# Linear attention followed by a gated long convolution, one core: more crossbar transposes, other eviction engines, shared buffer pools and a rewritten instruction order

## The chip, the cores and the metric

The program runs on one core of one Trainium2 chip. The metric is the device time of one execution in microseconds; the median of three runs of the kernel before is 264.32 us. Its profile is one execution recorded by the hardware profiler. The engines are TensorE (PE for its matmuls, PEld for its weight loads), VectorE (DVE), ScalarE (ACT), GpSimd (POOL) and the sync engine (SP); the last two mostly issue transfers here.

## What is computed

For 8 batches, 8 heads, 576 positions and a head size of 64, attention is replaced by positive random features; its output, with the heads side by side as 512 columns, goes into a gated convolution along the positions, done as a Fourier transform over 576 points:

```python
q_p, k_p = phi(q * scale), phi(k * scale)      # exp(x @ omega.T - |x|^2/2 - max) / sqrt(128)
kv  = einsum('bhsm,bhsd->bhmd', k_p, v)
z   = sum(k_p, axis=2)
num = einsum('bhsm,bhmd->bhsd', q_p, kv)
den = einsum('bhsm,bhm->bhs', q_p, z)[..., None] + 1e-06
x   = (num / den).transpose(0, 2, 1, 3).reshape(8, 576, 512)

x1, x2, x3 = split(x @ w_proj, 3)
conv = irfft(rfft(x2, axis=1) * rfft(filter, axis=0), n=576, axis=1)
out  = (x1 * conv * x3) @ w_out
```

## The kernel before

**Tiling.** A batch has 512 "main" positions, four blocks of 128, and 64 "left" positions; the left ones of two batches share a block of 128. The eight batches are so handled as four pairs. The function `attention` writes down the first half of the work for all batches, `hyena` the second half for all pairs. The 576-point Fourier transform is done by matmuls with tables of sines, after a fold that splits it into three.

**How one batch goes through.** Keys, queries and values come from DRAM through GpSimd's queue and are cast to bf16 on the way (`load_main`, `load_left`; tiles kn, qn, vn, kl, ql, vl). Keys and queries must be turned, so that the head dimension lies across partitions: kn becomes kt, qn becomes qt. There are two ways. Either TensorE multiplies 128x128 blocks with an identity, eight into one PSUM bank, and VectorE or ScalarE copies the bank out (`transposes`, `turn_keys`, `turn_queries`); or one DMA with transposition, issued on SP, moves the whole tile through the crossbar (`cross`). The table `CROSSED` (line 24) says from which batch on the second way is taken: 5 for keys, for queries and for the attention output. Then TensorE multiplies with omega and ScalarE takes the exponential (ek for keys, eqt for queries). VectorE takes each key row's maximum over the features and scales the values by it (`max_to_c`, `scale_values`; vc). TensorE sums keys times values to kv, multiplies the queries with it, VectorE divides (`normalise`; xb), and the result is turned back to xt: by TensorE and a ScalarE copy (`turn_back`, `turn_runs`), or through the crossbar.

**Second half.** xt is folded on VectorE (`fold`; xf), projected (`project2`, `gates`; tiles x and x13), transformed (`forward`; xs and sp, with `sw` and `xw` as copies whose partition halves are swapped by SP transfers), multiplied with the filter's spectrum (`spectrum`; ha, hb, hps, hqs), transformed back (yt) and multiplied with w_out; the results osb go out through SP.

**The filter.** It is loaded by GpSimd (`load_filter`), folded by seven VectorE additions and subtractions (`fold_filter`), transformed by TensorE (`filter_transform`) and put into place by SP transfers (`split_out`). The spectrum of the first batch needs it.

**Order.** Nothing is issued as it is written down. The class `Plan` records every operation; consecutive matmuls into the same tile form one. At the end `issue` (line 226) emits them in the order of the list of numbers `ORDER` (line 26), which fixes the order on each engine and in each transfer queue. Every engine works its own queue in order; a waiting instruction holds all behind it. GpSimd's queue has up to eight transfers under way: each waits for the one eight places ahead of it.

**Buffers.** Each tile name has its own ring of buffers in one of the pools `nat`, `att`, `hy` (qn 2, xt 4, x13 3, and so on); a tile that takes over a buffer waits until the last user of the former one is done. PSUM has eight banks: two pairs named a (`two_banks`), three single ones named h (`bank`) and one named t (`bank_t`) for transposes.

In the profile every instruction has line 232, the line that emits it, so groups are told apart by tile names.

Of the kernel before, what the change touches and what calls it, by code (L numbers as in the profile page):

```python
# [12 lines left out]
FP32 = mybir.dt.float32  # L13
BF16 = mybir.dt.bfloat16
# [7 lines left out]
P = 128  # L22

CROSSED = {"keys": 5, "queries": 5, "out": 5}

ORDER = """
    0 28 138 55 1 29 30 136 32 2 33 26 35 4 137 27 3 5 37 31 56 11 38 39 10 22 44 7 48 45 8 49 46
    50 6 40 52 15 23 51 34 24 84 13 139 41 42 20 47 70 43 21 71 36 77 69 85 25 9 53 86 54 73 57 72
    75 87 585 587 82 588 58 59 589 63 88 61 12 74 60 64 62 89 66 90 96 91 78 17 68 92 65 97 76 67
    93 98 95 80 211 586 107 99 106 109 100 142 148 108 110 81 79 149 112 101 150 154 94 14 152 102  # L30
    151 155 590 153 103 156 104 158 157 214 594 105 159 219 111 180 141 593 181 164 114 113 19 160
    165 16 115 182 161 116 184 117 162 183 118 122 163 18 119 123 120 222 124 216 121 125 210 126
    170 127 172 628 171 223 173 623 624 128 146 215 166 174 626 129 212 224 591 176 629 130 213
    592 140 167 644 226 175 596 597 595 625 630 131 627 168 177 225 144 132 169 637 645 133 651
    178 632 639 134 646 143 642 179 654 135 185 638 598 228 631 652 643 186 187 227 633 218 601
    599 640 655 229 188 641 602 191 189 603 192 600 647 193 605 650 604 190 635 194 606 607 195
    145 653 196 230 666 609 217 231 197 608 198 147 611 610 282 232 612 83 199 287 233 250 615 200
    613 201 205 251 202 616 617 252 614 203 619 206 204 618 207 288 621 620 289 253 718 254 208
    291 255 209 290 719 720 292 665 221 294 622 722 293 295 667 296 669 724 297 670 298 234 721
    671 347 235 299 656 236 246 237 304 673 247 659 305 674 248 306 672 681 307 286 249 683 238  # L40
    352 657 684 257 658 320 284 239 682 240 256 241 687 321 308 686 258 309 689 685 649 358 690
    260 648 359 688 663 242 244 259 243 661 245 691 350 262 264 692 662 660 694 318 265 664 357
    364 261 319 285 365 263 322 668 283 300 675 323 324 269 676 677 270 271 301 266 703 267 701
    268 704 693 274 678 272 275 702 276 277 679 707 273 636 278 279 709 634 708 696 280 710 705
    360 695 281 680 723 711 706 362 810 220 346 302 341 355 303 361 342 726 343 479 363 697 344
    353 367 811 345 366 829 813 699 368 351 424 725 370 348 698 815 814 700 356 728 712 371 738
    816 741 349 740 713 743 714 739 473 311 812 369 749 474 744 754 750 742 745 752 751 746 755
    313 817 753 756 310 818 747 314 382 757 312 727 758 716 316 315 782 386 317 785 729 783 715
    325 328 788 383 329 326 418 327 731 786 387 354 789 830 333 330 730 790 717 336 732 331 784
    337 334 338 734 332 335 426 736 388 372 733 339 428 735 389 340 390 427 791 391 373 881 429  # L50
    374 375 430 828 792 431 376 832 384 883 793 787 833 377 433 834 421 379 485 378 380 836 819
    432 423 737 400 420 835 434 837 419 846 385 820 844 748 759 435 847 450 760 451 436 850 845
    437 495 851 392 438 852 496 822 831 853 439 761 824 823 821 762 763 825 826 764 401 381 765
    854 827 477 771 394 448 855 476 766 773 475 857 772 838 767 768 774 856 839 769 776 449 452
    775 393 777 864 453 454 778 840 779 780 866 841 468 865 842 797 469 395 470 794 867 798 396
    868 397 795 471 849 800 472 848 872 869 801 562 398 796 882 799 873 886 843 884 399 802 858
    870 563 425 781 402 859 405 871 885 406 407 889 403 887 874 888 413 891 890 404 803 414 892
    878 408 893 770 409 415 410 894 895 860 862 804 411 913 412 805 861 416 879 915 806 417 863
    896 917 483 875 488 918 487 481 914 919 876 807 880 422 489 920 809 916 922 484 921 490 897
    923 482 877 491 899 924 898 925 480 493 928 900 478 931 929 926 440 930 441 933 932 442 939  # L60
    934 944 941 935 942 940 927 936 443 444 937 901 943 446 445 1008 945 961 903 486 1009 946 447
    950 947 953 989 962 458 455 951 459 992 963 938 456 952 990 457 902 993 954 991 461 994 460
    1007 464 462 995 996 463 465 955 466 997 497 904 467 492 905 494 948 956 906 498 957 808 964
    907 908 513 965 514 909 966 536 970 507 911 516 967 1011 508 910 968 1012 515 969 1060 912 971
    999 518 958 517 1062 1064 509 972 519 510 1015 1010 520 959 1013 1066 539 1016 538 1061 540
    976 1014 1063 541 949 973 998 1000 977 542 499 543 974 978 1001 500 544 501 502 504 1005 503
    511 1002 512 979 1006 545 1023 1003 1024 546 980 982 1004 981 960 547 1025 983 1029 506 548
    1026 1031 1030 505 1027 549 1019 1028 1032 550 521 537 1020 551 985 522 1033 526 984 986 560
    1038 1022 1034 975 1068 1037 561 1021 1039 523 1070 1017 524 527 525 1065 1018 528 529 1067
    532 1069 530 531 1072 533 534 552 1074 1036 535 553 1041 1073 554 1040 1071 1043 555 1042 1035  # L70
    1096 987 1075 1044 557 556 1098 1101 1097 1099 558 1102 1107 1100 1112 1109 1103 564 1108 1110
    559 1113 1045 1111 1049 565 1104 1114 1051 566 1115 1046 1105 567 570 1052 568 1047 1092 1116
    1050 988 1169 1140 569 1094 1048 1170 573 1141 1143 574 575 1142 1146 1168 571 580 572 1147
    1171 581 1148 582 576 1172 1173 577 578 583 1057 1174 1093 579 1144 1058 1149 1095 1175 1106
    1150 1187 584 1151 1076 1176 1188 1059 1077 1078 1053 1118 1079 1081 1120 1190 1119 1191 1080
    1186 1178 1177 1192 1082 1083 1194 1054 1084 1195 1055 1193 1056 1202 1179 1086 1204 1203 1121
    1205 1123 1122 1207 1129 1117 1124 1134 1206 1130 1131 1125 1132 1145 1135 1210 1133 1085 1136
    1211 1126 1137 1208 1087 1088 1127 1209 1189 1089 1090 1216 1128 1180 1091 1182 1138 1181 1212
    1158 1213 1152 1159 1139 1215 1183 1217 1160 1155 1153 1218 1184 1154 1156 1214 1157 1196 1185
    1198 1161 1199 1197 1201 1239 1162 1200 1164 1241 1163 1230 1165 1224 1231 1219 1222 1225 1220  # L80
    1228 1221 1223 1275 1226 1229 1280 1276 1167 1232 1240 1277 1227 1281 1278 1243 1279 1242 1244
    1245 1282 1283 1286 1246 1247 1287 1237 1288 1248 1249 1233 1251 1235 1234 1250 1271 1236 1252
    1273 1238 1253 1272 1254 1289 1274 1291 1290 1297 1292 1256 1299 1293 1298 1284 1255 1294 1295
    1259 1257 1258 1319 1285 1296 1325 1320 1261 1322 1328 1323 1326 1324 1300 1329 1302 1301 1330
    1308 1303 1313 1310 1327 1304 1260 1309 1166 1314 1311 1321 1262 1264 1305 1312 1263 1315 1307
    1316 1267 1306 1265 1318 1266 1268 1269 1331 1270 1317 1332 1335 1334 1333 1338 1336 1337 1341
    1339 1340 1344 1342 1343 1345 1346 1348 1347
# [148 lines left out]
def kernel(  # L236
# [39 lines left out]
    def bank():  # L276
        return nc.tile(psum, [P, 512], FP32, name="h", bufs=3)

    def bank_t():
        return nc.tile(psum, [P, 512], FP32, name="t", bufs=1)  # L280
# [4 lines left out]
    def load_main(b, which, parts=1, between=None):  # L285
        nc.at("load " + which, b)
        if which == "q" and b >= NS:

            t_ = nc.tile(nat, [P, NT, H, D], BF16, name="qn", bufs=2)
            nat_tiles[which, b] = t_  # L290
            for t in range(NT):
                nc.gpsimd.dma_start(
                    out=t_[:, t], in_=q[b, :, t * P : (t + 1) * P].rearrange("h s d -> s h d")
                )
            return
        src = {"q": q, "k": k, "v": v}[which]
        t_ = nc.tile(nat, [P, H, NT, D], BF16, name=f"{which}n", bufs=2)
# [11 lines left out]
    def load_left(i, which):  # L309
        nc.at("load " + which + "l", 2 * i)  # L310
        src = {"q": q, "k": k, "v": v}[which]
        t_ = nc.tile(nat, [P, H, D], BF16, name=f"{which}l", bufs=1)
        for j in range(2):
            nc.gpsimd.dma_start(
                out=t_[j * SL : (j + 1) * SL, :, :],
                in_=src[2 * i + j, :, SM:S, :].rearrange("h p d -> p h d"),
            )
        nat_tiles[which + "l", i] = t_
# [1040 lines left out]
```

The softmax here doesn't subtract the row's maximum and nothing guards it: scores larger than these inputs give would overflow.

## Time and profile before

| | |
|---|---|
| runs of the kernel before | 264.32, 263.89, 265.74 us; median 264.32 |
| span of the profiled execution | 264.5 us |
| granted TensorE clock, mean | 0.987 |
| DMA packets | 86786, 35.26 MB |
| GpSimd's queue (loads) | 59616 packets, 17.31 MB |
| SP's queue | 27000 packets, 17.47 MB |
| crossbar transposes | 9, some 4.4 us from issue to landing |
| loads of 512 KB by GpSimd | 8.2 to 11.5 us from issue to landing |
| ScalarE table loads | 2, 1283 ns each |

The busy time of an engine is the time in which one of its instructions ran; matmuls overlap, so that a TensorE that is always busy may still hold more or less work. The chain of waits follows back from the last instruction, at each step to what released it. In lists of groups, the numbers after the bar are the summed time, the mean of one instruction in ns, and the engine's idle time just ahead of them with what ended it. Times in the timeline are in us from the start of the span.

### The profile page before, as it was taken

How to read it: one execution, taken by the hardware profiler on the slowest of the kernel's cores; microseconds unless marked ns; L12 is line 12 of the kernel's file. 1: busy time of each engine (PE TensorE's matmuls, PEld its weight loads, DVE VectorE, ACT ScalarE, POOL GpSimd, SP SyncE). 2: the span in 40 equal slices, each digit the busy share in tenths (PEclk: the TensorE clock that was granted, in tenths of full speed). 3: DMA queues.
4: the chain of work that ended last, by engine and by line, in shares of the span. 5: the costliest groups of instructions: out<-in, count | busy, mean ns of one | idle time of the engine just before them, and what ended most of it. 6: DMA issues, size and time to landing. Idle time of an engine off the chain costs nothing.

```text
span 264.5 us, 5749 instructions
## 1 busy us (share of the span) xinstructions
PE 243.5 (92%) x2250; PEld 138.2 (52%) x2250; DVE 211.6 (80%) x474; ACT 194.0 (73%) x308; POOL 63.0 (24%) x88
## 2 busy tenths in 40 slices
PE   0665969999999999999999999999999999999994
PEld 0443836565476647655456454446456554456541
DVE  6896795689968999999399897599989889279480
ACT  4796579758999997987958967996495654763533
POOL 7865652902360912313017000000000000000000
PEclk9998699999999999999999999999999999999999
DMA  7999999999999999998579958416444511520136
GB/s 68 164 187 197 195 201 189 185 196 177 84 181 142 133 144 145 171 182 55 128 173 136 116 121 174 124 42 151 125 85 141 121 41 41 178 59 2 46 132 198
DMA packets 86786, 35.26 MB, mean 133 GB/s; under 512 B 58219, under 2 KB 81256, under 8 KB 86760
## 3 DMA queue, kind: packets, MB, share of 16 engines
q0 software_dynamic: 59616, 17.31, 64.2%
q1 hardware_dynamic: 27000, 17.47, 26.3%
q8 instruction: 17, 0.28, 0.4%
q10 hardware_dynamic: 144, 0.13, 0.1%
q14 instruction: 9, 0.07, 0.1%
HBM read 34.64 MB, written 9.44 MB: 167 GB/s over the span
## 4 chain that ended last, share of the span: by engine, by line
PE 77%; DMA 7%; DVE 6%; ACT 5%; issue 2%; POOL 1%; SPq 1%; DVEq 0%; POOLq 0%
PE h L232 60%; PE a L232 13%; PE t L232 4%; DMA vl<-in_v_dram 4%; DMA qn<-in_q_dram 3%; ACT ek L232 2%; SPq L232 1%; DVE x L232 1%; DMA xw<-xr 1%; DVE xb L232 1%; DVE kt L232 1%; ACT qt L232 1%; POOL kn L232 1%; ACT x L232 1%; DVE yt L232 1%
## 5 line engine op out<-in xcount | busy, mean ns | idle before, releaser
L232 PE MATMUL h<-xt,wproj 128*128 128x512 bf16 x256 | 62.8, 380 | 0.0
L232 ACT CAST x<-h 128x512 bf16<-128x512 f32 x68 | 40.0, 596 | 25.9 <-PE h L232 25.7
L232 PEld LDWEIGHTS <-wproj 128*128 128x128 bf16 x384 | 31.0, 98 | 25.5 <-issue 1.1
L232 ACT ACTIVATE eqt<-a 128x1024 bf16<-128x1024 f32 x32 | 32.2, 1040 | 3.5 <-PE a L232 3.5
L232 ACT ACTIVATE osb<-h 128x512 f32<-128x512 f32 (+4 forms) x49 | 27.2, 571 | 10.0 <-PE h L232 7.3
L232 ACT ACTIVATE ek<-a 128x1024 bf16<-128x1024 f32 x32 | 32.1, 1040 | 3.1 <-PE a L232 3.1
L232 POOL DMA_DIRECT2D qn<-in_q_dram x26 | 23.1, 894 | 40.4 <-PE t L232 16.0
L232 PE MATMUL h<-wproj,xf 128*128 128x512 bf16 x128 | 31.7, 379 | 0.0
L232 DVE TENSOR_TENSOR x<-h,x 128x512 bf16<-128x512 f32 x32 | 22.0, 687 | 11.8 <-PE h L232 10.1
L232 PE MATMUL h<-wout,yt 128*128 128x512 bf16 x128 | 30.9, 379 | 0.3 <-DVE yt L232 0.3
L232 DVE TENSOR_TENSOR bt<-h,osb 128x384 f16<-128x384 f32 x32 | 17.0, 551 | 6.7 <-PE h L232 6.1
L232 PEld LDWEIGHTS <-yt 128*128 128x128 bf16 x128 | 11.9, 98 | 14.1 <-DVE yt L232 1.0
L232 PE MATMUL h<-x,fwb 128*128 128x512 bf16 x72 | 18.7, 379 | 0.0
L232 PEld LDWEIGHTS <-xf 128*128 128x128 bf16 x134 | 12.2, 98 | 12.3 <-issue 0.2
L232 DVE TENSOR_TENSOR xb<-a,rden 128x512 bf16<-128x512 f32 x24 | 16.3, 688 | 0.5
L232 PE MATMUL h<-gtab,xs 128*128 128x384 bf16 x64 | 15.6, 326 | 0.1
L232 PE MATMUL a<-om,kt 64*128 64x128 bf16 x256 | 11.8, 226 | 3.7 <-DVE kt L232 3.7
L232 PEld LDWEIGHTS <-eqt 128*128 128x128 bf16 x256 | 11.4, 99 | 6.4 <-DVE xb L232 1.0
L232 PE MATMUL a<-kv,eqt 128*128 128x65 bf16 x256 | 12.6, 195 | 0.4 <-DVE xb L232 0.2
L232 PE MATMUL a<-qt,om 64*128 64x512 bf16 x64 | 11.4, 390 | 1.5 <-ACT ek L232 0.7
L232 PEld LDWEIGHTS <-kt 64*128 64x128 bf16 x256 | 7.8, 98 | 8.7 <-DVE kt L232 5.0
L232 PE MATMUL a<-vc,ek 128*128 128x65 bf16 x256 | 11.9, 200 | 0.0
(157 smaller groups left out, 475.8 us busy)
## 6 DMA issues: line engine op xcount, KB each, us to landing
out_dram<-osb SPq DMA_DIRECT2D x24, 256.0 KB, 2.3
vn<-in_v_dram POOLq DMA_DIRECT2D x8, 512.0 KB, 9.2
kn<-in_k_dram POOLq DMA_DIRECT2D x7, 512.0 KB, 8.7
qn<-in_q_dram POOLq DMA_DIRECT2D x24, 128.0 KB, 7.0
sw<-sp SPq DMA_DIRECT2D x16, 128.0 KB, 2.5
wproj<-in_moe_w_proj_dram POOLq DMA_DIRECT2D x3, 512.0 KB, 11.5
qn<-in_q_dram POOLq DMA_DIRECT2D x2, 512.0 KB, 8.2
out_dram<-xf SPq DMA_DIRECT2D x4, 256.0 KB, 2.2
```

Of the source, the lines that this page charges most:

```text
L232: getattr(real, name)(*args, **kw)
```

## The change

- `CROSSED` becomes 3 for keys and queries and 2 for the output: five batches of keys and queries and six of the output go through the crossbar instead of three each.
- All queries that TensorE still turns (batches 0, 1 and 2) are copied out of PSUM by ScalarE. Before, VectorE did it for batches 0 and 1.
- The seven additions and subtractions of `fold_filter` are issued on GpSimd instead of VectorE.
- The identity is made by VectorE, by comparing two ramps, instead of by GpSimd.
- The named rings of the pools are replaced by three shared rings: m4 (22 buffers of 4 KB per partition), m2 (10 of 2 KB) and m1 (19 of 1 KB). The bank t is given to h, which has four.
- `ORDER` is a new list, 1329 operations instead of 1349.

```diff
-CROSSED = {"keys": 5, "queries": 5, "out": 5}
+N4, N2, N1 = 22, 10, 19
+
+CROSSED = {"keys": 3, "queries": 3, "out": 2}
...
     def bank():
-        return nc.tile(psum, [P, 512], FP32, name="h", bufs=3)
+        return nc.tile(psum, [P, 512], FP32, name="h", bufs=4)
...
     def bank_t():
-        return nc.tile(psum, [P, 512], FP32, name="t", bufs=1)
+        return nc.tile(psum, [P, 512], FP32, name="h", bufs=4)
...
-        t_ = nc.tile(nat, [P, H, NT, D], BF16, name=f"{which}n", bufs=2)
+        t_ = nc.tile(hy, [P, H, NT, D], BF16, name="m4", bufs=N4)
...
         iota(si[:, 0 : 2 * CH], pattern=[[1, 2 * CH]], base=0, channel_multiplier=0)
-        nc.opaque("POOL", lambda: make_identity(tc.nc, ident[:]), ident[:], 650.0)
+        iota(fp[:], pattern=[[0, 1]], base=0, channel_multiplier=1)
+        nc.vector.tensor_scalar(
+            out=ident[:], in0=si[:, 0:P], scalar1=fp[:, 0:1], scalar2=None, op0=ALU.is_equal
+        )
...
-            nc.vector.tensor_tensor(out=x[:, o], in0=x[:, y], in1=x[:, z], op=op)
+            nc.gpsimd.tensor_tensor(out=x[:, o], in0=x[:, y], in1=x[:, z], op=op)
...
-                kt = nc.tile(att, [P, H, 2, P], BF16, name="kt", bufs=1)
-                qt = nc.tile(att, [P, NT, NPAIR, P], BF16, name="qt", bufs=1)
+                kt = nc.tile(hy, [P, H, 2, P], BF16, name="m4", bufs=N4)
+                qt = nc.tile(hy, [P, NT, NPAIR, P], BF16, name="m4", bufs=N4)
...
-                        b >= 2,
+                        True,
...
-                xt = nc.tile(hy, [P, CB, SM], BF16, name="xt", bufs=4)
+                xt = nc.tile(hy, [P, CB, SM], BF16, name="m4", bufs=N4)
```

All other tiles of one, two and four KB change their pool and name in the same way. In the instruction streams that result, TensorE has 2138 matmuls instead of 2250, VectorE no copies of turned queries, and GpSimd's queue has the filter's folds between its loads: four after the load of the filter's main part, the other three in places among the next twelve loads. SP's queue has the first five crossbar transposes (keys of batches 3 and 4, queries of 3, output of 2, keys of 5) ahead of or among the filter's placing and the first swaps.

## The prediction

> **What bounds the kernel now.** I read the page's busy table, slices and chain first, then busy time by stretch, then the chain in order of time, the groups kept apart by shape, and the queues.
>
> ```profile
> PE 243.5 (92%) x2250; PEld 138.2 (52%) x2250; DVE 211.6 (80%) x474; ACT 194.0 (73%) x308; POOL 63.0 (24%) x88
> PE   0665969999999999999999999999999999999994
> PE 77%; DMA 7%; DVE 6%; ACT 5%; issue 2%; POOL 1%; SPq 1%; DVEq 0%; POOLq 0%
> ```
>
> TensorE is full from the seventh slice (40 us) to the last, and 77% of the chain is its own. So there are two things to buy: less TensorE work, and an earlier moment from which it is full. By stretch (columns: stretch, length, PE, PEld, DVE, ACT, POOL busy, granted clock, DMA share, GB/s):
>
> ```profile
> 0.00:10.00 10.00, 1.01 (x6) 0.57 (x7) 7.43 (x32) 4.94 (x9) 8.67 (x20) 1.00 0.87 93
> 20.00:30.00 10.00, 6.99 (x103) 5.67 (x101) 6.41 (x13) 6.32 (x8) 5.82 (x8) 0.70 1.42 198
> 30.00:35.00 5.00, 3.76 (x54) 2.47 (x52) 4.55 (x11) 1.54 (x3) 2.54 (x4) 0.92 1.60 192
> 35.00:40.00 5.00, 3.83 (x31) 1.73 (x33) 4.92 (x17) 5.00 (x7) 2.94 (x4) 1.00 1.30 202
> 40.00:45.00 5.00, 4.99 (x80) 3.90 (x79) 2.25 (x4) 4.95 (x10) 1.77 (x2) 1.00 1.60 190
> ```
>
> Up to 40 us TensorE idles while VectorE is the busy engine (9.5 of the 10 us from 30 to 40) and the DMA engines move a steady 190 to 200 GB/s. Prices on TensorE come from the chain, start to start:
>
> ```profile
> 46.90 1.73 PE h L232 x8
> 76.90 0.46 PE t L232 x8
> 181.19 1.26 PE a L232 x40
> ```
>
> That is 216 ns for a product 512 columns wide, 56 for a transpose, 31.5 for one of 65. With 32.5 ns for key features (x8 0.26), 163 and 83 ns for 384 and 192 columns (timeline), the 2250 matmuls weigh 730 x 0.216 + 304 x 0.0555 + 640 x 0.0315 + 288 x 0.0325 + 128 x 0.0555 + 96 x 0.163 + 64 x 0.083 = 232.1 us. I call the clock minus the weight issued so far the **lag**. In this timeline
>
> ```profile
> 45.35 0.81 PE L232 MATMUL h<-wproj,xf 128*128 128x512 bf16 x3
> ```
>
> is the first projection; 20.2 us of weight stand ahead of it, so the lag is 25.1. The first output product (97.3) has 69.6 ahead: 27.7. The last (260.5) has 231.9: 28.6. The span is 232.1 + 28.6 + 3.8 of tail = 264.5, 0.2 from the runs' median of 264.32, so I use one for the other. Nearly all lag is made in the first 45 us.
>
> **What the skill says.** "TensorE: Matmul & The Clock Gate" (Wait — 56ns, not 53.3ns?) gives 55.6 and 215.7 ns from start to start at 128 and 512 columns, warm; the chain's 56 and 216 agree. "Advanced Engine Details and Errata" (X-Bar Transpose (TRN2)) calls crossbar transposes as fast as plain DMAs, 350 to 400 GB/s; the trace's take 4.4 us to land 512 KB, some 120 GB/s with their latency, and I use the trace. "GPSIMD Engine Reference" (3.1 Elementwise; 8. Key points) has a two-input add of 2048 fp32 at 4497 ns on GpSimd, and its SBUF interface shared with VectorE. No run here shows that; from it I estimate 1.12 us for 512 columns, more beside a busy VectorE.
>
> **The change, part by part.** *Transposes.* Keys and queries of batches 3 and 4, outputs of 2, 3 and 4 leave TensorE: seven sets of 16, 112 matmuls x 0.0555 = 6.2 us. TensorE is full there, so all counts: weight 225.9. Their evictions go too, off engines with room:
>
> ```profile
> L232 DVE COPY kt<-t 128x1024 bf16<-128x1024 bf16 x10 | 6.8, 684 | 1.4 <-PE t L232 1.4
> L232 ACT COPY qt<-t 128x1024 bf16<-128x1024 bf16 x6 | 6.3, 1056 | 0.0
> L232 DVE COPY qt<-t 128x1024 bf16<-128x1024 bf16 x4 | 2.7, 686 | 1.3 <-PE t L232 1.3
> L232 ACT COPY xt<-t 128x1024 bf16<-128x1024 bf16 x6 | 6.1, 1021 | 2.1 <-PE t L232 2.1
> L232 DVE TENSOR_TENSOR yt<-yt 128x512 bf16<-128x512 bf16 x5 | 2.0, 414 | 0.0
> ```
>
> VectorE loses 4 kt copies, 4 qt copies and 7 folds of 0.41: 8.4 us. ScalarE loses 6 xt copies, trades 4 late qt copies for 4 early ones.
>
> *Start.* Identity moves from GpSimd (TensorE's first wait, until 6.9) into VectorE's queue behind the residues: first transpose near 9.5. In the new stream ScalarE loads tables three times (1.28 each), one now behind a VectorE value. First exponential: 14.0, against 12.54. From there to the last turned block of batch 0 ScalarE has 17 exponentials x 0.90, 5 copies x 0.93, 9 short ones x 0.49 (chain and timeline spacings) = 24.4, plus about 1 waiting for the values of batch 0, which land some 3 us later in the new order: 39.5. The first third of wproj stands behind 5376 KB instead of 5056, so at 37 instead of 23.77 + 11.5 = 35.3. First projection at 40, with 18.1 ahead: lag 21.9, a gain of 3.2.
>
> *Filter fold.* In the new order TensorE's first filter product stands at weight 32.1 (54.0 at lag 21.9) and waits for the third of three folds on GpSimd. Their load has 2496 KB more ahead of it than wproj's third, at 190 GB/s 13.5 us: lands at 50.5. With f per fold it waits until 50.5 + 3f. While GpSimd waits and folds it issues no load. Behind stand six issues (5.2 us), a fold, an issue, the keys of batch 4, two folds, two issues, and the last piece of queries 3: issued at 50.5 + 6f + 8.6, landed 7.0 later (page), crossed 4.4 later, 70.5 + 6f; TensorE takes them at weight 55.7. So that path asks a lag of 14.8 + 6f: 21.5 at f = 1.12, 24.4 at 1.6, 28.3 at twice the estimate. VectorE is near full then; I take f = 1.6. Bounds: 0.8 (twice VectorE's 0.41; nothing excludes that it hides) and 2.25.
>
> *Crossings and SP.* Sixteen instead of nine, the first five of them (keys 3 and 4, queries 3, output 2, keys 5) among the filter's stores and the sw, xw swaps on SP:
>
> ```profile
> 88.93 6.56 SPq L232 DMA_TRANSPOSE kt<-kn  x1
> 133.06 1.87 SPq L232 DMA_TRANSPOSE qt<-qn  x1
> ```
>
> One held SP 6.6 us with GpSimd issuing, one 3.3, the later seven 1.3 to 2.2. Keys 4 can go at 70; at 3.3 each keys 5 are out near 83, then fifteen small moves x 0.6 end at 92, landing by 95; VectorE has them in its queue ahead of what TensorE wants at weight 72.9 (97). Covered, by 2 us; without that cover it is a stall of the excess.
>
> *Pools.* No instruction. They add waits: values 4 now wait for keys 5 to be crossed, a piece of queries 6 for TensorE at weight 83; both hold GpSimd's queue, values 4 land near 93 and are used after 110. One PSUM bank more for h, shared with t: ScalarE has one more to run ahead, I count nothing.
>
> Sum: 225.9 + lag + 3.8. The lag starts at 24.4; before, it still grew by 3.5 after the first projection, by waits on evictions and small gaps. I add 2, since part of that now hides in the fold's wait: **256.1**. With no growth and no wait 225.9 + 21.9 + 3.8 = 251.6; with f = 2.25 and 3 more, 261.
>
> **Rivals.** *The crossings take the gain back (no change).* If the first ones each hold SP 6.6 us because GpSimd is loading: keys 4 go at 70, output 2 leaves at 90 instead of being there at weight 58.7 (83): 7 us, lag 31.5 and 1 more, 262.2. For it: the 88.93 line, and a DMA share of 1.3 to 1.8. Against: the other eight took 3.3 or less.
>
> *GpSimd holds the loads (slower).* The same 14.8 + 6f: at f = 3.3 it asks 34.6, and 225.9 + 34.6 + 3.8 = 264.3, the point from which it decides; at f = 4, 38.8 and 268.5. For it: a queue in order, in front of all loads, and a VectorE 4.6 to 4.9 of 5 us busy. Against: it needs three times the page's price.
>
> *The new order does nothing for the start.* ScalarE is the only busy engine there; Some 3 us more there and the lag is 25.1 as before: 225.9 + 28.6 + 3.8 = 258.3, the transposes alone.
>
> **Numbers.** Forecast and the start rival, both faster: 0.72 and 0.09. Crossings, no change: 0.11. GpSimd, slower: 0.08. 1% is 2.6 us, about what a measurement tells from none. Range 251.5 to 263: from no growth to the crossings' case.
>
> **What will show it.** 2138 matmuls; first projection at 40 (45.35 before); TensorE waiting for GpSimd near 54; fold durations against 1.6; sixteen DMA_TRANSPOSE, the first six near 1.9 to 3.3 each; lag at the end below 28. Wrong if a stretch after 60 us shows TensorE idle by several us before kt, qt or xt.

## The result, and the profile after

The change makes the kernel **slower**: 268.85 us median (268.12 to 269.41 in three runs, 274.74 in the profiled one) against 264.12 us for the kernel before in the same session. The ratio is 1.0143, with a 95% interval of 1.0096 to 1.0191. The forecast was 256.1 us, with a range up to 263.

The lines of the page that answer to those shown of before, from the profiled execution of the kernel after:

```profile
PE 238.2 (87%) x2108; PEld 132.7 (49%) x2138; DVE 207.1 (76%) x460; ACT 190.1 (70%) x303; POOL 72.8 (27%) x94
PE   0477799988998929999966999999999999999993
PE 68%; DMA 10%; DVE 8%; ACT 8%; issue 2%; SPq 1%; ACTq 0%; DVEq 0%
```

That execution took 274.74 us at a mean clock of 0.965, so the readings below are from a second trace of the same kernel (run a0: 268.18 us, span 266.4, clock 0.977). Its slices of TensorE:

```profile
PE   0477799996999939999999899999999999999993
```

TensorE is full from the sixth slice on, one earlier than before, as wanted, but now the tenth slice (60 to 67 us) drops to 6 and the fifteenth (93 to 100 us) to 3. TensorE's share of the chain falls from 77% to 68 or 66%. A sum that is 6.2 us lighter takes longer because TensorE waits in the middle, where before every slice read 9. The stretches of run a0 (columns: stretch, length, PE, PEld, DVE, ACT, POOL busy, clock, DMA share, GB/s) give both ends of the story:

```profile
35.00:40.00 5.00, 5.00 (x88) 3.85 (x86) 2.90 (x6) 4.83 (x8) 2.29 (x4) 1.00 1.24 205
...
60.00:65.00 5.00, 2.95 (x11) 0.94 (x9) 4.94 (x8) 2.89 (x4) 5.00 (x5) 0.80 1.74 162
95.00:100.00 5.00, 0.25 (x2) 0.00 (x0) 0.96 (x2) 1.56 (x3) 2.41 (x3) 1.00 1.39 222
```

From 60 to 65 us VectorE (4.94) and GpSimd (5.00) are both full while TensorE has 2.95. From 95 to 100 us no engine is: they wait for something that is not an engine.

The forecast's own measure, the lag (clock minus TensorE's weight so far; where the trace misses matmuls, the program's list is used, so that these figures hold to some 0.3 us), puts a size on each part:

| | before | forecast | after (a0) |
|---|---|---|---|
| first projection (45.35; after 40.3 us) | 25.1 | 21.9 | 22.2 |
| at 60 us | 26.1 | 24.4 | 23.8 |
| at 70 us | 27.1 | | 27.9 |
| at 90 us | 27.7 | | 29.3 |
| at 110 us | 28.5 | | 35.6 |
| last output product | 28.6 | 26.4 | 36.0 |

225.9 + 36.0 + 4.5 of tail = 266.4, against 256.1. At 60 us the change was ahead of its forecast. Then it lost 4.1 us near 63, 1.4 between, and 6.3 near 100.

**The first loss.** VectorE and GpSimd in the timeline of run a0 (columns: start, duration, engine, operation, count, and the idle time ahead with what ended it):

```profile
53.17 2.69 DVE L229 TENSOR_TENSOR m<-m 128x1024 bf16<-128x1024 bf16 x2
...
60.47 1.63 DVE L229 TENSOR_TENSOR vcl<-m,vcl 64x512 bf16<-64x512 bf16 x1
```

```profile
50.25 5.33 POOL L229 TENSOR_TENSOR m<-m 128x512 bf16<-128x512 bf16 x3 [3.48 <-DMA m<-in_moe_filter_fft_dram]
...
60.61 1.21 POOL L229 TENSOR_TENSOR m<-m 128x512 bf16<-128x512 bf16 x1
```

The GpSimd lines are filter folds. The VectorE lines are ordinary work, and they are too long: the first line is two operations, one of 1024 columns and one of 512 (a line shows the shape of its first), which take 1.03 us in e4, not 2.69; the multiplication of the left values takes 0.42, not 1.63. Note 1.63 = 0.42 + 1.21: it took its own time plus one fold on GpSimd. TensorE then waits for VectorE:

```profile
59.61 1.04 PE L229 MATMUL h<-wproj,m 128*128 128x512 bf16 x4
62.70 1.63 PE L229 MATMUL h<-wproj,m 128*128 128x512 bf16 x4 [2.05 <-DVE m L229]
64.12 1.91 PE L229 MATMUL h<-m,wproj 128*128 128x512 bf16 x4
```

Four products take 1.04 us ahead of the gap, and 1.63 and 1.91 behind it. The wait is 2.05 us long by the profile's ends of matmuls, and 2.2 counted from the four products' weight, 4 x 0.216; both counts occur below, some 0.2 us apart. The lag grows by 4.1.

**The second loss.** SP's queue and ScalarE, same run:

```profile
72.19 12.18 SPq L229 DMA_TRANSPOSE m<-m  x3
84.42 0.58 SPq L229 DMA_DIRECT2D hps<-m  x1
85.11 2.18 SPq L229 DMA_TRANSPOSE m<-m  x1
...
91.49 1.31 SPq L229 DMA_DIRECT2D hqs<-m  x2
...
98.16 0.60 SPq L229 DMA_DIRECT2D hqs<-m  x1
```

```profile
98.44 0.58 ACT L229 CAST m<-h 128x512 bf16<-128x512 f32 x1 [5.36 <-DMA hqs<-m]
```

Four crossbar transposes hold SP from 72 to 87 us, and the filter's placing (hps, hqs) stands between and behind them until 98.8. ScalarE waits 5.36 us for it: its copy takes over a buffer of the shared ring m2 that the placing still reads. VectorE waits 3.97 us, because its products need hps. Behind ScalarE's copy stands the last exponential of the queries, and so TensorE idles 4.75 us up to 100.0. The move that ScalarE waits for is the second of the two issued from 91.49 us on; it landed at 98.3, some 6 us later. The pages say the same of such moves (medians from issue to landing, of the kernel before and of run a0):

```profile
hqs<-osb SPq DMA_DIRECT2D x4, 64.0 KB, 6.2
hqs<-m SPq DMA_DIRECT2D x4, 64.0 KB, 6.0
```

### The profile page after: what moved, and what is told of

Its sections match the earlier page's. It is cut to its first block, busy times and chain, and to the rows that moved or that the text cites. A ratio compares the mean times of both kernels' runs of the same rounds, so it can differ in the third digit from the quotient of the medians.

```text
span 273.0 us, 5512 instructions
## 1 busy us (share of the span) xinstructions
PE 238.2 (87%) x2108; PEld 132.7 (49%) x2138; DVE 207.1 (76%) x460; ACT 190.1 (70%) x303; POOL 72.8 (27%) x94
## 3 DMA queue, kind: packets, MB, share of 16 engines
q1 hardware_dynamic: 41560, 21.14, 34.2%
## 4 chain that ended last, share of the span: by engine, by line
PE 68%; DMA 10%; DVE 8%; ACT 8%; issue 2%; SPq 1%; ACTq 0%; DVEq 0%
PE h L229 57%; PE a L229 11%; DMA m<-m 8%; DVE m L229 6%; ACT ek L229 3%; DMA hqs<-m 2%; ACT m L229 2%; ACT eqt L229 2%; SPq L229 1%; DVE vcl L229 1%; ACT L229 0%; DVE rden L229 0%; DVE eql L229 0%; DVE mx L229 0%; ACT kv L229 0%
## 5 line engine op out<-in xcount | busy, mean ns | idle before, releaser
L229 ACT CAST m<-h 128x512 bf16<-128x512 f32 (+1 forms) x132 | 72.1, 583 | 48.0 <-PE h L229 40.1
L229 PEld LDWEIGHTS <-m 128*128 128x128 bf16 (+2 forms) x983 | 71.0, 101 | 67.1 <-DVE m L229 14.8
L229 PE MATMUL h<-m,wproj 128*128 128x512 bf16 (+1 forms) x373 | 74.6, 335 | 4.7 <-DMA m<-m 4.3
L229 ACT ACTIVATE m<-h 128x512 f32<-128x512 f32 (+4 forms) x57 | 32.2, 570 | 13.6 <-PE h L229 12.2
L229 PE MATMUL h<-wproj,m 128*128 128x512 bf16 x138 | 37.4, 391 | 2.3 <-DVE m L229 2.0
L229 POOL DMA_DIRECT2D m<-in_q_dram x34 | 28.7, 860 | 27.1 <-DVE bt L229 20.6
L229 PE MATMUL h<-wout,m 128*128 128x512 bf16 x136 | 35.0, 384 | 0.7 <-issue 0.3
L229 DVE TENSOR_TENSOR m<-m 128x512 bf16<-128x512 bf16 (+3 forms) x52 | 27.2, 533 | 5.7 <-DMA m<-m 4.7
L229 DVE TENSOR_TENSOR m<-h,m 128x512 bf16<-128x512 f32 x36 | 24.5, 681 | 7.6 <-PE h L229 7.3
L229 POOL DMA_DIRECT2D m<-in_v_dram x16 | 12.7, 798 | 45.8 <-PE h L229 25.1
L229 DVE TENSOR_TENSOR bt<-h,m 128x384 f16<-128x384 f32 x32 | 16.9, 553 | 10.4 <-ACT m L229 8.6
L229 DVE TENSOR_TENSOR m<-a,rden 128x512 bf16<-128x512 f32 x36 | 24.2, 684 | 0.6
```

Source lines behind the costliest of these rows:

```text
L229: getattr(real, name)(*args, **kw)
```

## The experiments

Ratios are to the kernel before, timed beside each; 0.38% is 1 us. All kernels start from the kernel after unless another is named.

| run | ratio | 95% interval |
|---|---|---|
| a0 | 1.0162 | 1.0096 to 1.0228 |
| e1_fold_vector | 1.0185 | 1.0115 to 1.0255 |
| e2_moves_off_sp | 1.0109 | 1.0078 to 1.0141 |
| e3_queries5_first | 1.0213 | 1.0139 to 1.0288 |
| f1_no_more_crossings | 1.0346 | 1.0309 to 1.0384 |
| f3 (f1, with e1 and e2) | 1.0397 | 1.0354 to 1.0440 |
| g1_late_pieces | 1.0299 | 1.0265 to 1.0334 |
| b1_before_fold_gpsimd | 1.0248 | 1.0211 to 1.0285 |
| b2_before_queries_scalar | 1.0010 | 0.9990 to 1.0031 |
| e4_fold_vector_later | 1.0113 | 1.0034 to 1.0192 |
| h2 (e4 and e2) | 1.0068 | 1.0023 to 1.0114 |
| h1 (h2 and g1) | 0.9923 | 0.9889 to 0.9957 |
| h1 again | 0.9915 | 0.9880 to 0.9949 |
| d1 (h1 and idle work on GpSimd) | 1.0036 | 1.0011 to 1.0060 |
| i1 (h1, two edits) | 0.9996 | 0.9956 to 1.0037 |
| i2 (i1, one more) | 0.9978 | 0.9950 to 1.0006 |
| i3 (i2 without i1's moved folds) | 0.9875 | 0.9814 to 0.9935 |
| i4 (h1 and i2's edit) | 0.9985 | 0.9956 to 1.0015 |

**a0: does it belong to the kernel?**

> The changed kernel once more, for a trace whose granted clock is near 1. If the three idle stretches of TensorE seen in its first trace (2.2 us near 60 us before a projection that waits for VectorE, 5.3 near 95 us before sums that wait for ScalarE, 4.4 near 140 us behind a crossbar transpose) belong to the kernel, they are here again within 1 us and the time is 268. If they came with the low clock of that execution (0.965), they are gone and the time is below 262.

The first two stretches are there again, 2.2 and 4.9 us counted from the weights. The third is not: it came with that execution, and nothing below explains it.

**b1: the fold alone, in the kernel before.**

```diff
-            nc.vector.tensor_tensor(out=x[:, o], in0=x[:, y], in1=x[:, z], op=op)
+            nc.gpsimd.tensor_tensor(out=x[:, o], in0=x[:, y], in1=x[:, z], op=op)
```

> The kernel before with its seven filter folds on GpSimd and nothing else changed. Theory, a fold there takes 1.2 to 1.8 us and VectorE's bf16 work beside it 1.3 us instead of 0.4, in a stretch in which VectorE is full, and the loads behind the folds are later: 266 to 270. Rival, the fold hides: 263.5 to 265.

271.17 us, 6.6 more by the ratio: one word costs more than the whole change does. The timelines of VectorE, GpSimd and TensorE in this run:

```profile
38.01 4.49 DVE L232 TENSOR_TENSOR vc<-vn,vc 128x2048 bf16<-128x2048 bf16 x1 [0.42 <-DMA vn<-in_v_dram]
```

```profile
38.21 1.17 POOL L232 TENSOR_TENSOR yt<-yt 128x512 bf16<-128x512 bf16 x1
...
40.02 1.16 POOL L232 TENSOR_TENSOR x<-x 128x512 bf16<-128x512 bf16 x1
...
41.83 2.79 POOL L232 TENSOR_TENSOR yt<-yt 128x512 bf16<-128x512 bf16 x2
```

```profile
41.23 0.59 PE L232 MATMUL h<-x,fwar 128*128 128x512 bf16 x1 [4.16 <-POOL x L232]
```

TensorE waits 4.16 us for a fold, and VectorE's scaling of the values takes 4.49 us where its group has a mean of 1.22 in the kernel before. So two prices lie on top of each other: the fold's result comes late, and VectorE is held. The next two experiments part them.

**e1 and e4: the folds back on VectorE.** In e1 at the same places of `ORDER`; in e4 four of them (603, 606, 605, 607) behind operation 580.

```diff
-            nc.gpsimd.tensor_tensor(out=x[:, o], in0=x[:, y], in1=x[:, z], op=op)
+            nc.vector.tensor_tensor(out=x[:, o], in0=x[:, y], in1=x[:, z], op=op)
```

> The seven filter folds go back to VectorE, at the same places of the order. Theory one, the folds on GpSimd cost twice, once by slowing VectorE's bf16 work beside them (1.3 us instead of 0.41 for 512 columns) and once by holding the loads of keys 4 and 5 behind them: VectorE's work is at its usual durations, the keys of batch 4 are issued some 5 us earlier, the idle stretch near 60 us is gone and the one near 95 us is shorter; 261 to 265. Rival, the crossings on SP's queue set the second stretch and the first is only moved: 267 to 269.

> The folds on VectorE again, but four of them (the three of the first rows and the one of the middle rows) stand later in its order, where the filter has landed, so that VectorE does not wait for it with the products of the gates behind. Theory, the fold on GpSimd costs what the 1.3 us bf16 operations beside it cost, some 4 us of VectorE's time before 63 us, and the earlier try gave that back by waiting 3.2 us for the filter: no idle stretch over 1 us before 66 us, the lag at 70 us is 25 instead of 27.9; the stretch near 100 us stays, since SP's queue sets it, so the time falls by 0 to 3 us, 266 to 269. Rival, VectorE's total work sets the lag at 70 us, which stays near 27.

e1 gains nothing: VectorE waits 3.19 us for the filter's load at 50.99 us, and TensorE 2.77 us for VectorE behind it. The load of keys 4 was issued no earlier than 60.4 us (62.6 in a0), since its buffer was not free; that half of the theory fell. In e4 that wait is gone too. The operations shown for a0 above now read

```profile
53.87 1.03 DVE L229 TENSOR_TENSOR m<-m 128x1024 bf16<-128x1024 bf16 x2
...
58.74 0.42 DVE L229 TENSOR_TENSOR vcl<-m,vcl 64x512 bf16<-64x512 bf16 x1
```

The same run of VectorE's work, from the fold of ek to the reciprocal of vc, takes 7.1 us (52.54 to 59.62) instead of 11.35 (51.22 to 62.57). One part of the 4.3 us, 0.77 at 57.90, stands in a0 beside issues of loads on GpSimd and not beside a fold. But such issues alone stretch nothing: in before, e1, e4, h2 and both runs of h1, which have them without folds on GpSimd, no operation of VectorE is over 0.25 us longer than the median of its kind. How that one part comes about is open. The gap near 63 us is gone, the lag at 71.5 us is 25.4 (of which 1.8 is a new wait for two later folds). The gap near 96 us stays, 3.6 us, as expected. In time the two intervals still overlap; the trace, not the clock, shows this step.

**d1: work on GpSimd that nobody waits for.** Kernel h1 (below, all folds on VectorE) with fourteen subtractions of 256 columns on GpSimd near the folds' former places; what they write is not used.

```diff
+    for _ in range(14):
+        nc.gpsimd.tensor_tensor(out=idle[:], in0=wproj[:, 0, 0:256], in1=wproj[:, 1, 0:256], op=ALU.subtract)
```

> The kernel with the late pieces (262.7; folds on VectorE, moves on GpSimd), plus fourteen subtractions of 256 columns on GpSimd, bf16, near where the change had its seven folds; they read a constant and nobody uses what they write, so TensorE waits for none of them. Theory, GpSimd's elementwise work by itself slows VectorE's bf16 operations beside it: these take 1 us or more longer where the two meet near 46 to 58 us, TensorE waits for VectorE again before 66 us and the time rises by 2 to 5 us, to 265 to 268. Rival, the change lost there only because TensorE waited for the folds' results: no operation of VectorE is longer, and the time stays at 262 to 263.5.

1.0036 against 0.9923, intervals apart: 1.13%, 3.0 us, for results that nobody reads. VectorE's five operations of 512 columns, in h1 and then in d1, and GpSimd beside them:

```profile
50.77 1.88 DVE L229 TENSOR_TENSOR m<-m 128x512 bf16<-128x512 bf16 x5
```

```profile
51.37 3.18 DVE L230 TENSOR_TENSOR m<-m 128x512 bf16<-128x512 bf16 x5 [0.66 <-DMA m<-in_moe_filter_fft_dram]
```

```profile
46.75 6.84 POOL L230 TENSOR_TENSOR idle<-wproj 128x256 bf16<-128x256 bf16 x8
```

TensorE then waits for VectorE at 59.3 (1.9 us) and 63.4 (1.4 us), which it doesn't in h1. The delay of loads behind the idle work is in the 3.0 us too; the stretched operations show that it isn't all. The Trainium skill, "SBUF — State Buffer" (SBUF: two separate sides), names a mechanism: the SBUF port pair that VectorE and GpSimd share is an exclusive lock; of GpSimd's operation and a VectorE operation with two SBUF inputs, whichever starts first has it for the whole instruction, and "the other fully blocks". The traces agree that the two don't run side by side: the 1.63 = 0.42 + 1.21 above is such a block, and a VectorE operation with one input in PSUM took its usual 0.68 us beside the idle work (at 49.19). That the first one holds the ports to its end they do not show: by the recorded starts, VectorE's instruction at 38.01 us in b1 began ahead of three folds, was held by all three, and two of them took no longer than alone (1.17 and 1.16 us).

**e2 and h2: the filter's placing off SP's queue.** The thirteen moves are issued by GpSimd, behind the load of keys 5 (the last four behind operation 611). h2 is this on top of e4.

```diff
-            nc.sync.dma_start(out=dst[rows, c, :], in_=sc_[of, x, :])
+            nc.gpsimd.dma_start(out=dst[rows, c, :], in_=sc_[of, x, :])
```

> The thirteen small moves that place the filter are issued by GpSimd, which stands idle then, and no longer stand behind four crossbar transposes on SP's queue. Theory, the moves come too late because SP is held by transposes of 4 us each: the 5.3 us near 95 us go, 262 to 264. Rival, the values of batch 4, which wait for the crossed keys of batch 5, or the sums themselves set that stretch: 267 to 269.

> The last kernel, and the filter's small moves issued by GpSimd. Theory, with both causes gone (VectorE slowed beside GpSimd, SP's queue) the lag ends at 31 to 32, set by the crossings of keys 4, queries 3 and output 2 at 72 to 86 us: 262 to 264. Rival, VectorE's or another limit brings it back to 34 to 36: 266 to 269.

In both, the stretch near 96 to 100 us is gone, ScalarE's wait for hqs with it. But both gain little: TensorE now waits for turned keys 4 and queries 3 at 82 and 86 us (e2: 1.4 and 1.9 us, with 0.9 more for output 2 at 90; h2: 2.6 and 2.5 us). Those crossings start at 72 (h2: 69) us, and the first three hold SP for 2.9 to 6.4 us each. One wait had covered the next. h2's lag ends at 31.2, as its theory said.

**g1 and h1: buffers taken too early.** `ORDER` loads one of the four pieces of queries 7, 5 and 4 long before the others. Each piece takes one of the 22 buffers of m4. They go to their siblings (462 behind 459, 344 behind 84, 282 behind 338); then, by the theory, keys 4 wait for an earlier reader, and values 4 no longer for the crossed keys of 5. h1 is this on top of h2.

> Three pieces of queries, of batches 7, 5 and 4, each of which takes one of the 22 common buffers long before its other three pieces are loaded, are loaded with those. Keys 4 then wait for no late reader, and the values of 4 no longer wait for the crossed keys of 5. Theory, these early pieces starve the loads of buffers: keys 4 are issued and crossed earlier than at 72 us, the idle stretch near 100 us shrinks by 2 us or more; 264 to 267. Rival, the stretch is SP's queue alone: 267 to 269.

> The last kernel, and the three early pieces of queries loaded with their siblings, so that the loads of keys 4 and queries 3 are issued some 5 us earlier. Theory, the crossings then start at 67 instead of 72 us and the lag ends at 28 to 30: 259 to 262. Rival, the crossings themselves, of 4 us each, or the later pieces set it: 263 to 268.

> The kernel with the late pieces again, on another chip, beside the two that follow: 0.99 of the kernel before, 261.5 to 263.5 where that takes 264 to 265. If its gain was that chip's, it is at 1.00.

Alone it makes things worse (272.6 us): the placing on SP still ends at 99.7 us, and the gap there grows to 6.2. On top of the other two it brings h1 from 1.0068 to 0.9923, 3.8 us, with the intervals apart: 262.67 us, and 262.45 on another chip. h1 beats both kernels. Its slices, from the second run (span 260.7):

```profile
PE   0476799999799999899998989999999999999991
```

The lag of the second run is 25.2 at 100 us and 28.9 at the end, that of the first 26.4 and 31.9; in the first, a wait of 2.3 us for crossed queries at 110 us takes back what was won. The gain in time is shown, its way is not the theory's. In the first run keys 4 are loaded from 51.2 us on instead of 56.7 (h2), but land only 0.5 us earlier, and the first of the four crossings starts at 68.4 (66.7 in the second run) instead of 69.0. What changed more is the crossing itself: it lands 9.4 us after its issue instead of 12.5, and h2's waits at 82 and 86 us are gone. Why it is shorter was not tested.

**f1 and f3: no more crossings than before.** f1 has the old `CROSSED`; the added transposes stand four TensorE operations ahead of their first reader.

```diff
-CROSSED = {"keys": 3, "queries": 3, "out": 2}
+CROSSED = {"keys": 5, "queries": 5, "out": 5}
```

> The changed kernel with only the crossings of the kernel before: keys, queries and outputs of batches 3 and 4 (outputs from 2) are turned on TensorE again, the other parts of the change stay. 112 transposes come back, 6.2 us of TensorE's work. Theory, the early crossings cost more than that, since each holds SP's queue for 4.1 us with the filter's moves behind it: the idle 4.9 us near 100 us and the slow products after it go, the lag of TensorE ends near 28.5 instead of 36.0, and the time is 264 to 266. Rival, the idle stretches come from the new order and the common buffers: the lag stays near 36 and the time is 271 to 274.

> As the last, and in addition the folds on VectorE and the small moves of the filter issued by GpSimd. If each of the three parts costs on its own, the lag ends at 26 to 28 and the time is 262 to 265. If the earlier idle stretch near 53 to 63 us is VectorE's total work, whoever folds, it is as the last kernel, within 1 us.

The theory fell: f1 takes 273.3 us. The gap near 100 us is gone and the lag ends at 34.2, but 6.2 us of transposes are back. In this order, with the transposes put where they were, the added crossings are worth 1.8 to 2.0% of the time, about 5 us of the 6.2 they remove, net of the second loss, which they bring; what loses on balance is the rest. f3 is no better; with e1's placing of the folds VectorE waits for the filter here too (2.9 us, and TensorE behind it 2.7, up to 52.5 us).

**e3, b2 and the refinements of h1.**

> The last three loads of the queries of batch 5 stand ahead of the piece of queries 6 whose buffer comes free only at 119 us. Theory, that wait holds GpSimd's queue for 20 us, so the queries of 5 and, behind them on SP, the output of batch 4 are crossed late, which is the 4.4 us near 140 us: these go, 263 to 265. Rival, the crossings after 100 us are slow by themselves (6 us each beside the loads): the stretch stays and the time is 267 to 269.

> The kernel before with all turned queries evicted by ScalarE, nothing else changed: four copies of 0.69 us leave VectorE, four of 1.05 us go to ScalarE before 40 us. Theory, ScalarE is the busy engine at the start, so the first projection comes 1 to 3 us later and the time is 265 to 267. Rival, VectorE bounds the start and it gains: 261 to 263.5.

> The kernel with the late pieces (262.7), with the queries of 5 loaded ahead of the piece of queries 6 and the two folds of the rest rows earlier on VectorE. Its lag grew at 71.5 us (1.8, a filter product that waits for VectorE), at 110 (2.3, queries 4 not yet crossed) and 145 (1.9). Theory, the first of these is those two late folds and the last comes from GpSimd's queue, held 15 us by the piece of queries 6: the lag ends at 28 to 29, 258.5 to 261. Rival, other work takes their place: 262 to 263.5.

> The last kernel, with the four moves of the filter's rest rows back on SP, where they come after the crossed keys of 5. On GpSimd they wait 6.8 us for ScalarE with the loads of values 4, keys 6 and queries 4 behind them. Theory, that wait is why queries 4 are crossed late at 110 us: the 2.3 us there go, and the time is 1.5 to 2.5 us below the last kernel. Rival, the crossing of queries 4 waits for its place in SP's queue: no difference over 0.7 us.

> The kernel with the late pieces, with the four rest moves on SP and the queries of 5 ahead of the piece of queries 6, and the two rest folds left where they were (moved earlier, they made VectorE wait for their load: 3.3 us at 60 us). Theory, the 2.3 us at 110 us and the 1.9 us at 145 us of the late pieces' kernel go with the queue of GpSimd: lag 28 to 29.5, 259 to 261. Rival, the crossings or ScalarE take their place: within 1 us of the late pieces' kernel.

> The kernel with the late pieces, with only the four rest moves back on SP. Theory, GpSimd's wait of 6.8 us for ScalarE delays the loads of queries 4: the stretch at 110 us shrinks by 1 us or more, 260.5 to 262. Rival, no difference over 0.7 us.

e3: no gain is seen from taking other loads ahead of GpSimd's wait of 21 us for one piece's buffer. b2: who copies the turned queries makes no difference. i1 and i2 moved two folds so early that VectorE waits 2.8 us for their load (i2) and TensorE 3.3 to 3.5 us for VectorE, which took back whatever the other edits brought. i3 (0.9875) can't be told from h1. i4 is worse than h1 by 0.6 to 0.7%, against its theory. Where it loses can be seen: in i3 and i4 alike VectorE waits again (3.2 and 4.5 us near 95 us) ahead of a product with hps, and TensorE behind it for 2.9 and 3.0 us in two parts; h1 has neither wait. i3 is i4 with e3's edit and lies 1.1% below it, so in that setting the edit may pay.

## Why the prediction was wrong, by its own steps

- **Transposes** (6.2 us): right. 2138 matmuls; f1 shows some 5 us of it in the time.
- **Start** (first projection at 40, lag 21.9): right, and by the steps it named; 40.3 and 22.2, with the first exponential at 13.9 us (14.0) and the first third of wproj landed at 37.3 (37). The rival "the new order does nothing for the start" is out.
- **Filter fold**: the size was right, the price was not. f = 1.6 against a mean of 1.54 over the seven; TensorE was to wait for the third fold until 50.5 + 3f = 55.3 us, and did so until 55.6. (The lag of 24.4 came from the path of queries 3, which were there only at 84.9, at a lag of 29.2, since their crossing took 10.0 us to land, not 4.4; other waits covered all but 0.7 us of that.) The step charged the fold to GpSimd's queue and to TensorE only, though it wrote "its SBUF interface shared with VectorE" two paragraphs above and used it for the fold's own duration. **This is the first step that failed:** it left out what a fold does to VectorE, which was full. e4 shows the size, 4.3 us more for the same VectorE work, to save 7 x 0.41, and d1 that it needs no result anybody waits for. TensorE's lag grows by 4.1 us near 63 us.
- **GpSimd holds the loads** (slower from f = 3.3): right sign, wrong mechanism. f was half of that, and e1's load of keys 4 was issued only 2.2 us earlier without folds on GpSimd.
- **Crossings and SP**: **the second step that failed,** by its cover. Keys 4 were to go at 70 us and keys 5 to be out near 83, at 3.3 us each, small moves until 92, "covered, by 2 us". Measured: 72.2, 87.3 and 98.8; the four take 2.2 to 5.4 us, and the moves 11.4 us instead of 9. The landing was sized too small besides: "end at 92, landing by 95" allows 3 us, where the page of before has 6.2 for such moves. With that, the sum's own 92 gives 98.2, behind the reader at 97: no cover at all. The reader was put at weight 72.9. It is at 66.3, since ScalarE's copy, with the queries' last exponential behind it, needs the placed buffer too. Forecast as "a stall of the excess", it was 4.9 us, plus slow products.
- **Pools** ("No instruction. They add waits"): the third. Of the waits it named, the piece of queries 6 is not seen to cost anything in the kernel after (e3). Two that were not followed do cost: ScalarE's copy into a ring buffer that SP still reads, and the early pieces, 3.8 us once the other two are mended, by a way that is not settled (h1).
- **The rival "the crossings take the gain back"** had the right place, and at 31.5 nearly the lag that h2 shows. That the numbers are so near is in part luck: h2 crosses with the moves off SP and the folds on VectorE. By itself the rival came to 262.2; the fold was missing in it.
- **Lag growth** (2 us from 60 us on): it was 12.2, and 10.4 of that are the two losses (4.1 and 6.3); the rest, 1.8, is near what was forecast.

What stays open: how far the shared rings as such, or the new order alone, would win or lose. They were not taken apart.

## What to carry to other kernels

Before moving elementwise work from VectorE to GpSimd, look at what VectorE does at that moment: here it saved VectorE seven operations of 0.41 us, 2.9 in all, and made seven others 6.1 us longer (a0, up to 67 us). When a queue gets new long transfers, list the small ones behind them and every engine that needs their buffers, not only their data. And expect a chain of covers: three causes here hid each other, each mended alone gained 0.5% at most, within the noise, or lost, and together they gave 2.2 to 2.5%.

## What the runs showed of the hardware that was not expected

A gap of TensorE costs more than its length. In a0 the third product after the gap at 62.7 us slows, and then products of 512 columns start 427 ns apart instead of 216: 1.9 us lost behind a gap of 2.2. The profile's granted clock is 0.50 there, from 63.0 to 66.4 us. From 35 us to the last products, every gap of at least 3.6 us (the second loss in a0, e1, e3, e4 and g1; b1 at 41 us) has such a stretch of 3.4 or 6.8 us beside it, with 1.8 to 2.6 us lost behind the gap. Of gaps of 2.0 to 3.5 us some have one (a0; h1 at 110 us; g1 at 64 us; i1 at 61 us), some none (e1 with 3.0 us at 53, e2, f3, h2, i2, i3). Below 2.0 us it was seen once, in i4, behind gaps of 1.7 and 1.3 us that stand close together.

The Trainium skill, "TensorE: Matmul & The Clock Gate" (What's actually happening), has this as a gate that halves the clock after an idle window of about 3.4 us and opens after as long a busy one, on a window that runs freely. The stretches of 3.4 us agree, and so do the 427 and 216 ns with the 426.7 and 215.7 of its section "Wait — 56ns, not 53.3ns?". That a gap of 2.2 us sometimes suffices does not: it is shorter than the window. What decides between the gaps of 2.0 to 3.5 us is not shown.
